# One flat list of single-engine steps in a new order, with every PSUM bank named by its step, for a windowed attention that feeds a gated two-layer MLP

## The chip, the cores and the metric

The kernel runs on one core of a Trainium2 chip. The metric is the device time of one execution in microseconds. Several runs are given by their median. A profile is one execution by itself; its span runs from its first to its last instruction.

## What is computed

Eight batches of eight heads, 576 positions and 64 columns a head. Each position attends to itself and the 63 before it. The result, 4608 tokens of 512 columns, goes through two matrices with a gated activation between them.

```python
scores = scale * np.matmul(q, k.transpose(0, 1, 3, 2))
mask = (rel >= 0) & (rel < 64)             # rel = query position - key position
attn = softmax(np.where(mask, scores, -1e9))
x = np.matmul(attn, v).transpose(0, 2, 1, 3).reshape(B * S, H * D)
h = x @ w_in                               # 512 -> 2048
g = h * (1.0 / (1.0 + np.exp(-1.702 * h)))
return (g @ w_out).astype(np.float32)      # 2048 -> 512
```

## The kernel before

**Units of work.** A block m (0 to 35) is 128 tokens, two groups of 64 queries. A chunk is four blocks. For a block: `scores` (L319) multiplies q and k of all heads into PSUM, `exp` (L333, L335) is ACT's, `mask` (L339) is DVE's, `pv` or `pv_two` (one block or two, L347) multiplies by v, `norm` (L363, L365) or `norm_two` (L391, L392) divides on DVE and writes `xs`. `xs` is then turned into `xT`: up to block 15 by TensorE (`x_mm`, `x_mm_two`) and a copy on ACT, from block 16 on by a DMA transpose on SP's queue (`x_dma`, L437).

**The MLP.** An up unit (`up_mm`, L453) takes w_in and `xT` and fills one PSUM bank: four groups of 128 features by 128 tokens up to chunk 2, two by 256 after. It is emptied by one gelu on ACT (`up_gelu`, L484) or by a tanh on ACT and a product on DVE (`up_th` L464, `up_g` L479). Chunk 0 goes down by plain products (`down`, L491). Every later half chunk q (2 to 17) goes down in seven products of a Winograd form of Strassen's scheme, each of eight matmuls (`product`, L568). Products 1, 6, 7 and 4 add up in one bank, the chain, which is copied out after 1, 6 and 7 (`keep_chain`, L113) before the next may write; products 2, 5 and 3 use a second bank, each followed by an add into the output tile (`add_out`, L593); `last_of_chain` copies the chain's end. Sums of gT and of w_out are made by DVE (`add_g` L544, `add_w` L528). Chunk 8 does its up part with the same scheme (`up_product` L668, `up_keep`, `up_add` L685, `up_last` L694, sums in `add_u` L635 and `add_x` L645).

**Transfers.** Batches 0, 1 and part of 2 come as fp32, are cast by POOL, DVE or ACT, and q and k are turned by TensorE or, in batch 2, by DMA. From (2, 3) on `load_bf16` (L228, L229) loads q, k and v with a cast from POOL's queue; `turn_dma` (L240) turns q and k into qt and kt on SP's queue; `shift_v` (L233, L235) makes a copy of v shifted by 64 rows on POOL, and waits for the v it copies. `store` (L584) writes an output tile, on SP's queue for the first twelve half chunks.

**Order.** The schedule is manual: each engine executes its instructions in the order in which the program makes them, and each step waits for its operands and buffers. Up to chunk 1 the order is Python calls written out; after that a text `plan` is read step by step, a letter and numbers each. Several letters stand for steps of several engines: `u32.g` is an up unit and its gelu, `l3.0` three loads, `y2.3` two transposes, `h2.3` two shifts, `t10` the transposes of a block pair with both copies. The queue of a store follows from the half chunk.

**Banks and buffers.** Eight PSUM banks: S (two), T (two), H (two, taken in turn) and O (two, taken in turn). In the plan up units use H, products O; `pv_two` takes one H bank for its eighth head; scores marked `.h` use both H banks. Output tiles come from one pool of five buffers in turn.

Of the kernel before, what the change touches and what calls it, by code (L numbers as in the profile page):

```python
# [29 lines left out]
def kernel(  # L30
# [20 lines left out]
    ob_pool = ctx.enter_context(tc.tile_pool(name="ob", bufs=5))  # L51
    psS = ctx.enter_context(tc.tile_pool(name="psS", bufs=1, space=bass.MemoryType.PSUM))
    psT = ctx.enter_context(tc.tile_pool(name="psT", bufs=1, space=bass.MemoryType.PSUM))
    psH = ctx.enter_context(tc.tile_pool(name="psH", bufs=2, space=bass.MemoryType.PSUM))
    psO = ctx.enter_context(tc.tile_pool(name="psO", bufs=2, space=bass.MemoryType.PSUM))
# [30 lines left out]
    def load_v(b, i, queue=None):  # L86
        (queue or nc.sync).dma_start(
            out=heads(stage_of_v(b, i)[0 : size(i), :]), in_=rows_of(v, b, i)
        )

    def cast_v(b, i, engine=None, parts=(0, 1, 2)):
        n, vn, vo = size(i), v_nat[b % 2], v_off[b % 2]
        src = heads(stage_of_v(b, i)[:])
        pieces = [
            (vo[64:128, i, :, 0:D], src[0:64]),
            (vn[0:n, i, :, 0:D], src[0:n]),
            (vo[0:64, i + 1, :, 0:D], src[64:128]) if i < 4 else None,
        ]
        for p in parts:
            if pieces[p]:  # L100
                (engine or nc.gpsimd).tensor_copy(out=pieces[p][0], in_=pieces[p][1])
# [4 lines left out]
    def load_qk(b, i):  # L106
        for w, src in enumerate((q, k)):
            nc.sync.dma_start(
                out=heads(stage_of_qk(b, i)[0 : size(i), w, 0:DM]), in_=rows_of(src, b, i)
            )  # L110
# [4 lines left out]
    def cast_qk(b, i):  # L115
        n = size(i)
        for w in range(2):
            nc.gpsimd.tensor_copy(
                out=rows[b % 2][w][0:n, i, :], in_=stage_of_qk(b, i)[0:n, w, 0:DM]
            )  # L120

    def load_quads(half):
        hs = slice(4 * half, 4 * half + 4)
        for w, src in enumerate((q, k)):
            nc.sync.dma_start(
                out=stage_qk[half][:, w, :].rearrange("p (h e) -> p h e", h=4),
                in_=src[0, hs, 0:512, :].rearrange("h (p r) d -> p h (r d)", r=4),
            )
# [37 lines left out]
    def load_pairs(b, i):  # L166
        n = pairs(i)
        for w, src in enumerate((q, k)):
            nc.sync.dma_start(
                out=stage_qk[(3 * b + i) % 2][0:n, w, :].rearrange("p (h e) -> p h e", h=H),  # L170
                in_=src[b, :, 256 * i : 256 * i + 2 * n, :].rearrange(
                    "h (p r) d -> p h (r d)", r=2
                ),
            )
# [17 lines left out]
    def turn_mm(b, i, w, tiles):  # L192
        n = pairs(i)
        for hp in range(4):
            for r in range(2):
                nc.tensor.transpose(  # L196
                    out=tiles[hp // 2][:, w, hp % 2, r, 0:n],
                    in_=pair_rows(b, i, w)[0:n, hp // 2, r, P * (hp % 2) : P * (hp % 2) + P],
                    identity=ident[0:n, 0:n],
                )  # L200

    def turn_out(b, i, w, tiles, half, engine):
# [6 lines left out]
            in_=tiles[half][:, w, :, :, 0:n].rearrange("p g r n -> p g n r"),  # L209
        )  # L210

    def turn_tiles():

        return [
            pool.tile([P, 2, 2, 2, P], bf16, name="turn", tag=tag)
            for pool, tag in ((psS, "S"), (psT, "T"))
        ]

# [7 lines left out]
    def load_bf16(b, i):  # L226
        for w, src in enumerate((q, k)):
            nc.gpsimd.dma_start(out=heads(row_block(b, i, w)), in_=rows_of(src, b, i))  # L228
        nc.gpsimd.dma_start(out=v_nat[b % 2][0 : size(i), i, :, 0:D], in_=rows_of(v, b, i))  # L229

    def shift_v(b, i):
        vn, vo = v_nat[b % 2], v_off[b % 2]
        nc.gpsimd.tensor_copy(out=vo[64:128, i, :, :], in_=vn[0:64, i, :, :])  # L233
        if i < 4:
            nc.gpsimd.tensor_copy(out=vo[0:64, i + 1, :, :], in_=vn[64:128, i, :, :])  # L235

    def turn_dma(b, i):
        n = size(i)
        for w in range(2):
            nc.sync.dma_start_transpose(  # L240
                out=qkt[b % 2][w][:, :, PAD + P * i : PAD + P * i + n],
                in_=row_block(b, i, w),
            )
# [15 lines left out]
    for half in range(2):  # L259
        load_quads(half)  # L260
    for i in (0, 2):
        load_v(0, i)
    ident = keep.tile([P, P], bf16, name="ident")
    nc.gpsimd.memset(ident[:], 0.0)
    nc.gpsimd.affine_select(
        out=ident[:], in_=ident[:], compare_op=ALU.not_equal, fill=1.0,
        base=0, pattern=[[-1, P]], channel_multiplier=1,
    )
    band = keep.tile([P, 64], bf16, name="band")
    nc.gpsimd.memset(band[:], 1.0)  # L270
    nc.gpsimd.affine_select(
        out=band[:], in_=band[:], compare_op=ALU.is_ge, fill=0.0,
        base=64, pattern=[[1, 64]], channel_multiplier=-1,
    )
    nc.gpsimd.affine_select(
        out=band[:], in_=band[:], compare_op=ALU.is_ge, fill=0.0,
        base=-1, pattern=[[-1, 64]], channel_multiplier=1,
    )
    for i in range(2):
        nc.vector.memset(qkt[i][1][:, :, 0:PAD], 0.0)  # L280
        nc.vector.memset(v_off[i][0:64, 0, :, :], 0.0)
        nc.vector.memset(v_nat[i][:, :, :, D : D + 2], 2.0)
        nc.vector.memset(v_off[i][:, 1:5, :, D : D + 2], 2.0)
        nc.vector.memset(v_off[i][64:128, 0, :, D : D + 2], 2.0)

    band_all = keep.tile([P, 1024], bf16, name="band_all")
    nc.vector.tensor_copy(
        out=band_all[:].rearrange("p (n c) -> p n c", c=64),
        in_=band[:].unsqueeze(1).to_broadcast([P, 16, 64]),
    )  # L290
    far = keep.tile([P, 512], bf16, name="far")
    nc.vector.tensor_scalar(
        out=far[:], in0=band_all[:, 0:512],
        scalar1=-1.0, scalar2=30000.0, op0=ALU.add, op1=ALU.mult,
    )
# [6 lines left out]
    def scores(m, masked=False, apart=False):  # L302

        if apart:
            st = [psH.tile([P, 512], fp32, name="S", tag="H")[:] for _ in range(2)]
# [67 lines left out]
    def pv_two(m):  # L373

        acc = psT.tile([P, 2, 512], fp32, name="Tacc", tag="T")
        rest = psH.tile([P, 2, 66], fp32, name="Tacc", tag="H")
# [27 lines left out]
    def x_dst(m):  # L404
        ch = m // 4
        if m % 4 == 0:
# [21 lines left out]
    def x_out_two(m):  # L428
        ps = X_of.pop(m)
        for i in range(2):  # L430
            nc.scalar.copy(out=x_dst(m + i), in_=ps[:, i])

    def x_out(m):
        nc.scalar.copy(out=x_dst(m), in_=X_of.pop(m)[:])
# [7 lines left out]
    turns = itertools.count()  # L442

    def up_mm(ch, f, nf, t0, nt, wide=False):

        pool, tag = (psO, "O") if wide and next(turns) % 2 else (psH, "H")
        ps = pool.tile([P, nf, nt], fp32, name="hps", tag=tag)

# [37 lines left out]
    def down(ch, tsub, j, pool=None, tag="O"):  # L486

        if j == 0:
            O_of[ch, tsub] = (pool or psO).tile([P, DM], fp32, name="ops", tag=tag)
# [9 lines left out]
    def down_out(ch, tsub, on_dve=False):  # L499
        o_sb = ob_pool.tile([P, DM], fp32, name="o_sb", tag="o_sb")  # L500
        ps = O_of.pop((ch, tsub))
        if on_dve:
            nc.vector.tensor_copy(out=o_sb[:], in_=ps[:])
        else:
            nc.scalar.copy(out=o_sb[:], in_=ps[:])
        eng = nc.sync if ch < 6 else nc.scalar
        eng.dma_start(out=out_tiled[:, ch * 4 + tsub, :], in_=o_sb[:])
# [40 lines left out]
    def bank(c, pr, at, name):  # L548
        pool, tag = (psO, "O") if (c, pr) != (NCH - 1, 1) else ((psS, "S"), (psT, "T"))[at]
        return pool.tile([P, 256], fp32, name=name, tag=tag)  # L550

    def product(c, pr, n):
# [8 lines left out]
        if n == 1:  # L561
            A_of[c, pr] = bank(c, pr, 0, "chain")
        if n == 2:
            C_of[c, pr] = bank(c, pr, 1, "part")
# [11 lines left out]
    def out_half(c, pr, t, n):  # L576
        if (c, pr, t) not in o_of:
            o_of[c, pr, t] = ob_pool.tile([P, DM], fp32, name="o_sb", tag="o_sb")
        return o_of[c, pr, t][:, 256 * n : 256 * n + 256]

    def store(c, pr, t, half=None):
        eng = nc.sync if c < 6 or half == 1 else nc.scalar
        cols = slice(0, DM) if half is None else slice(256 * half, 256 * half + 256)
        eng.dma_start(  # L584
# [6 lines left out]
    def add_out(c, pr, n):  # L591
        at, t, half = {2: (0, 0, 0), 5: (2, 1, 1), 3: (1, 0, 1)}[n]
        nc.vector.tensor_tensor(  # L593
            out=out_half(c, pr, t, half), in0=C_of[c, pr][:], in1=kept(c, pr, at), op=ALU.add
        )

    def last_of_chain(c, pr, engine):
        copy_on(engine, out=out_half(c, pr, 1, 0), in_=A_of.pop((c, pr))[:])
# [49 lines left out]
    rings = itertools.count()  # L648
    homes = {32: "ST", 33: "H", 34: "ST", 35: "H"}

    def up_bank(g, at):
        pool, tag = (psH, "H") if homes[g] == "H" else ((psS, "S"), (psT, "T"))[at]
        return pool.tile([P, 2, 256], fp32, name="up", tag=tag)[:]

    def up_product(g, n):
# [523 lines left out]
```

The softmax here doesn't subtract the row's maximum and nothing guards it: scores larger than these inputs give would overflow.

## Time and profile before

| what | value |
|---|---|
| runs | 295.73, 296.1 and 293.69 us, median 295.73 |
| the profiled execution | span 293.0 us; what lies around the span is not recorded |
| granted TensorE clock | 0.998 of full speed |
| first down product | 33.4 us |
| last matmul ends | 289.7 us |
| DMA packets | 149768, of which 135136 under 512 B; 42.79 MB |

Busy time is given by engine: PE is TensorE's matmuls, PEld its weight loads, DVE VectorE, ACT ScalarE, POOL GpSimd, SP SyncE, which here only issues transfers. A q behind a name means the sequencer of that engine. Groups are named by line, engine, operation and tiles; a wait is named by who waited and who ended it.

### The profile page before, as it was taken

What the parts mean: (1) busy time and instruction counts of PE and PEld (TensorE: products, weight loads), DVE (VectorE), ACT (ScalarE), POOL (GpSimd) and SP (SyncE); (2) the same over time, 40 slices, a digit from 0 to 9 for tenths busy, and PEclk for the clock granted to TensorE, in tenths of its full rate; (3) what the DMA queues carried; (4) which work ended last, traced back from release to release, by engine and by line L of the source; (5) the groups of instructions that cost most, each with busy time, mean ns of one, the idle gap of its engine ahead of it and who ended that gap; (6) DMA issues with size and microseconds to landing.
All of it is one profiled execution on the core that took longest, in us unless ns stands there. A gap on an engine that the chain in (4) does not pass through costs nothing.

```text
span 293.0 us, 8976 instructions
## 1 busy us (share of the span) xinstructions
PE 283.5 (97%) x3783; PEld 249.6 (85%) x3783; DVE 195.5 (67%) x377; ACT 181.1 (62%) x289; POOL 141.3 (48%) x191
## 2 busy tenths in 40 slices
PE   7899999999999999999999999999999999999995
PEld 6578555999898898889898999998899899989984
DVE  5667715898898685375636573756787864768771
ACT  3676534877775389776758746776657653556411
POOL 1570446744999999709569985078510000000000
PEclk9999999999999999999999999999999999999999
DMA  7999999996999999999999999999955171001233
GB/s 237 236 206 219 240 243 225 239 159 128 84 142 119 166 130 134 185 164 146 140 186 154 139 151 198 183 160 143 142 70 117 36 182 39 0 2 72 74 125 126
DMA packets 149768, 42.79 MB, mean 146 GB/s; under 512 B 135136, under 2 KB 144864, under 8 KB 149728
## 3 DMA queue, kind: packets, MB, share of 16 engines
q0 software_dynamic: 77712, 13.64, 70.7%
q1 hardware_dynamic: 68208, 25.18, 49.4%
q10 hardware_dynamic: 3808, 3.41, 3.7%
q8 instruction: 29, 0.48, 0.7%
q14 instruction: 11, 0.09, 0.1%
HBM read 36.70 MB, written 9.44 MB: 157 GB/s over the span
## 4 chain that ended last, share of the span: by engine, by line
PE 78%; DMA 10%; DVE 4%; ACT 2%; SPq 2%; issue 2%; POOL 1%; ACTq 0%; DVEq 0%; POOLq 0%
PE hps L453 32%; PE chain L568 17%; PE part L568 13%; PE ops L491 5%; PE up L668 4%; DMA out_dram<-o_sb 3%; PE Tacc L347 3%; PE S L319 3%; DMA kt<-rows_k 3%; DMA stage_v<-in_v_dram 2%; DMA stage_qk<-in_k_dram 2%; SPq L240 1%; DVE stage_qk L528 1%; ACT PT L335 1%; PE turn L196 1%
## 5 line engine op out<-in xcount | busy, mean ns | idle before, releaser
L453 PEld LDWEIGHTS <-w_in_sb 128*128 128x128 bf16 x1312 | 109.6, 113 | 4.9 <-issue 0.7
L484 ACT ACTIVATE gT<-hps 128x512 bf16<-128x512 f32 x82 | 48.6, 597 | 34.5 <-PE hps L453 34.2
L453 PE MATMUL hps<-xT_pe,w_in_sb 128*128 128x128 bf16 (+2 forms) x800 | 61.0, 234 | 0.1
L453 PE MATMUL hps<-xT_dma,w_in_sb 128*128 128x256 bf16 x512 | 60.6, 273 | 0.3 <-ACT gT L694 0.3
L568 PEld LDWEIGHTS <-gT 128*128 128x128 bf16 x512 | 49.0, 98 | 5.9
L479 DVE SCALAR_TENSOR_TENSOR gT<-th,hps 128x512 bf16<-128x512 bf16 x46 | 30.8, 684 | 11.2 <-ACT th L464 11.0
L233 POOL COPY v_off<-v_nat 64x528 bf16<-64x528 bf16 x27 | 20.2, 752 | 33.9 <-DMA v_nat<-in_v_dram 33.1
L464 ACT ACTIVATE th<-hps 128x512 bf16<-128x512 f32 x46 | 27.0, 600 | 13.0 <-PE hps L453 12.6
L593 DVE TENSOR_TENSOR o_sb<-part,stage_v 128x256 f32<-128x256 f32 x48 | 20.2, 421 | 21.9 <-PE part L568 13.3
L335 ACT ACTIVATE PT<-S 128x1024 bf16<-128x1024 f32 x28 | 28.5, 1017 | 8.0 <-PE S L319 7.6
L339 DVE TENSOR_TENSOR PT<-PT,band_all 128x1024 bf16<-128x1024 bf16 x32 | 23.6, 748 | 5.6 <-ACT PT L335 5.4
L229 POOL DMA_DIRECT2D v_nat<-in_v_dram x27 | 23.5, 871 | 0.8 <-DMA rows_q<-in_q_dram 0.5
L228 POOL DMA_DIRECT2D rows_k<-in_k_dram x27 | 23.3, 865 | 0.3 <-DMA v_nat<-in_v_dram 0.3
L228 POOL DMA_DIRECT2D rows_q<-in_q_dram x27 | 23.1, 856 | 0.0
L568 PEld LDWEIGHTS <-sums 128*128 128x128 bf16 x192 | 18.6, 98 | 3.2 <-issue 1.1
L568 PEld LDWEIGHTS <-stage_v 128*128 128x128 bf16 x192 | 18.5, 98 | 2.2
L113 ACT COPY stage_v<-chain 128x256 f32<-128x256 f32 x22 | 8.2, 372 | 18.3 <-PE chain L568 18.3
L392 DVE TENSOR_TENSOR xs<-Tacc,rc 128x128 bf16<-128x128 f32 (+1 forms) x26 | 18.0, 692 | 0.9
L113 DVE COPY stage_v<-chain 128x256 f32<-128x256 f32 x26 | 10.9, 420 | 11.1 <-PE chain L568 10.9
L235 POOL COPY v_off<-v_nat 64x528 bf16<-64x528 bf16 x21 | 17.2, 820 | 1.2
L568 PE MATMUL chain<-stage_qk,sums 128*128 128x256 bf16 x128 | 16.6, 273 | 0.3 <-DVE stage_v L113 0.3
L568 PE MATMUL chain<-stage_qk,gT 128*128 128x256 bf16 x128 | 16.6, 273 | 0.0
(127 smaller groups left out, 450.6 us busy)
## 6 DMA issues: line engine op xcount, KB each, us to landing
out_dram<-o_sb SPq DMA_DIRECT2D x24, 256.0 KB, 4.7
rows_q<-in_q_dram POOLq DMA_DIRECT2D x21, 128.0 KB, 6.3
rows_k<-in_k_dram POOLq DMA_DIRECT2D x21, 128.0 KB, 6.7
v_nat<-in_v_dram POOLq DMA_DIRECT2D x21, 128.0 KB, 7.4
out_dram<-o_sb ACTq DMA_DIRECT2D x10, 256.0 KB, 2.1
stage_v<-in_v_dram SPq DMA_DIRECT2D x9, 256.0 KB, 6.7
stage_qk<-in_q_dram SPq DMA_DIRECT2D x4, 512.0 KB, 6.9
stage_qk<-in_k_dram SPq DMA_DIRECT2D x4, 512.0 KB, 8.0
```

The source lines that it names most:

```text
L113: (nc.scalar.copy if engine is nc.scalar else engine.tensor_copy)(**kw)
L228: nc.gpsimd.dma_start(out=heads(row_block(b, i, w)), in_=rows_of(src, b, i))
L229: nc.gpsimd.dma_start(out=v_nat[b % 2][0 : size(i), i, :, 0:D], in_=rows_of(v, b, i))
L233: nc.gpsimd.tensor_copy(out=vo[64:128, i, :, :], in_=vn[0:64, i, :, :])
L335: nc.scalar.activation(out=e[:], in_=st[:], func=AF.Exp, scale=scale)
L339: nc.vector.tensor_tensor(out=pt, in0=pt, in1=band_all[:], op=ALU.mult)
L453: nc.tensor.matmul(ps[:, g, :], lhsT=w_in[:, c, (f + g) % 4 : 512 : 4], rhs=xT[ch][:, m0 : m0 + nt // P, c, :], start=(c == 0), stop=(c == 3),
L464: nc.scalar.activation(out=th[:], in_=ps[:], func=AF.Tanh, scale=1.702)
L479: nc.vector.scalar_tensor_tensor(out=g_of(*unit), in0=th[:], scalar=1.0, in1=ps[:], op0=ALU.add, op1=ALU.mult,)
L484: nc.scalar.activation(out=g_of(*unit), in_=ps[:], func=AF.Gelu_apprx_sigmoid, scale=2.0)
L568: nc.tensor.matmul(out[:, :], lhsT=left[:, j], rhs=right[:, j], start=new and j == 0, stop=j == 7, skip_group_check=True,)
L593: nc.vector.tensor_tensor(out=out_half(c, pr, t, half), in0=C_of[c, pr][:], in1=kept(c, pr, at), op=ALU.add)
```

## The change

The whole order, start included, becomes one text of 1291 steps, each of one engine (a transposing step, a load of q alone, one half of a shift, one copy). The order up to the first down product is that of before; from there on it is new. The H and O pools become four pools of one bank each, a to d, and each step that starts a bank says which. The five output buffers become five pools e to i, named by the step that first writes a tile. Queues of stores and engines of copies are named too. Each step does the arithmetic that it did before; where a gelu and where a tanh with a product empties an up unit is chosen anew.

```diff
-    ob_pool = ctx.enter_context(tc.tile_pool(name="ob", bufs=5))
+    ob0 = ctx.enter_context(tc.tile_pool(name="ob0", bufs=1))
...
+    obs = {"e": ob0, "f": ob1, "g": ob2, "h": ob3, "i": ob4}
-    psH = ctx.enter_context(tc.tile_pool(name="psH", bufs=2, space=bass.MemoryType.PSUM))
-    psO = ctx.enter_context(tc.tile_pool(name="psO", bufs=2, space=bass.MemoryType.PSUM))
+    psA = ctx.enter_context(tc.tile_pool(name="psA", bufs=1, space=bass.MemoryType.PSUM))
...
+    pools = {"S": psS, "T": psT, "a": psA, "b": psB, "c": psC, "d": psD}
-    def up_mm(ch, f, nf, t0, nt, wide=False):
-        pool, tag = (psO, "O") if wide and next(turns) % 2 else (psH, "H")
-        ps = pool.tile([P, nf, nt], fp32, name="hps", tag=tag)
+    def up_mm(ch, f, nf, t0, nt, tag):
+        ps = pools[tag].tile([P, nf, nt], fp32, name="hps", tag=tag)
-    def shift_v(b, i):
+    def shift_v(b, i, part):
-    def turn_dma(b, i):
+    def turn_dma(b, i, w):
-    def load_bf16(b, i):
+    def load_bf16(b, i, which):
-    def store(c, pr, t, half=None):
-        eng = nc.sync if c < 6 or half == 1 else nc.scalar
+    def store(c, pr, t, half, queue):
-        "t": turn,
-        "c": lambda m, *apart: scores(m, apart=bool(apart)),
+        "X": lambda m, tag: x_mm(m, pools[tag], tag),
+        "XX": lambda m, tag: x_mm_two(m, pools[tag], tag),
+        "Y": lambda m, e: x_out(m, engines[e]),
+        "YY": lambda m, i, e: x_out_two(m, i, engines[e]),
+        "xd": x_dma,
```

In the new text `u.6.12.2.256.256.d` is an up unit (chunk, feature group, groups, first token, tokens, bank), `e` its gelu, `t` and `g` its tanh and product; `p.11.1.a` a product; `k`, `o`, `z` its copies and add; `v.26.2.a` the attention product of two blocks; `n` the norm; `c` scores (two letters: banks apart), `x` exp, `m` mask; `XX` transposes on TensorE, `YY` their copies, `xd` a DMA transpose of xs; `lb` a load, `y` a DMA transpose of q (0) or k (1), `h` half a shift, `s` a store, `a` a sum of gT. Three places of before and after: block pair 12 up to its transposes, block pairs 14 and 16, and from block pair 26 to the first up unit that uses it.

```diff
-        a3.2 a3.4 c12 x12 p2.4 o2.5 p2.3 z2.V p3.1 o2.3 h3.3 k3.1.V m12 p3.2 o3.2 h3.4 c13 x13 p3.6
-        k3.6.A p3.5 p3.7 m13 y3.4 k3.7.V o3.5 v12 c14 p3.4 z3.A x14 n12 p3.3 t12 p4.1 c15 x15 y4.0
+        m.13 v.12.2.a z.2.A.g n.12.2 p.3.4 p.2.5 XX.12.T y.3.4.1 y.3.4.0 o.3.5.h y.3.3.1 z.3.V
+        lb.4.0.q YY.12.0.V o.2.5 YY.12.1.A y.3.3.0 c.14 c.15.ac x.15 y.4.0.1 x.14 p.3.3 a.5.3 p.2.3
...
-        m15 s2.0 s3.0 m14 c16 x16 v14 n14 m16 c17.h x17 l4.2 p4.5 p4.6 k4.6.V t14 m17 u54.g p4.7 v16
-        n16 c18 l4.3 t16 h4.0 l4.4 u55.g u56.g u57.g u58.g k4.7.V o4.5 u59.t g59 u60.g p4.3 o4.3
+        h.3.1.1 e.3.10.0 h.3.3.0 e.3.4.0 e.3.8.0 k.4.1.A c.17.ca c.16 x.17 s.2.0.N.S v.14.2.d n.14.2
+        h.3.4.0 y.4.0.0 p.4.6 u.3.12.2.0.256.d lb.4.3.k k.4.6.V y.4.1.1 XX.14.T YY.14.0.V p.4.2.c
...
+        u.3.0.2.256.256.b m.17 o.4.2.e u.3.12.2.256.256.a x.16 m.16 y.4.4.0 h.3.3.1 v.16.2.d
+        lb.4.2.q e.3.12.0 a.6.3 a.6.1 y.4.3.1 c.18 z.4.A.i a.6.2 a.5.2 y.4.2.0 e.3.6.256 lb.4.3.v
+        e.3.2.256 s.3.0.N.S e.3.0.256 h.4.4.0 e.3.12.256 c.19.ba x.19 lb.5.2.k n.16.2 p.4.5 xd.16
+        xd.17 o.4.5 lb.4.1.v s.4.1.N.S p.5.1.d k.5.1.A y.4.3.0 m.19 u.3.14.2.256.256.b t.3.14.256
+        g.3.14.256 p.5.6 k.5.6.V u.3.8.2.256.256.a t.3.8.256 g.3.8.256 p.4.3 o.4.3 p.5.7 k.5.7.V
...
-        y7.1 y7.0 k9.6.V u97.g u98.g m28 l7.2 p9.7 k9.7.A u99.g o9.2 v26 l7.3 s5.1 a10.1 n26 y6.3
-        c29 a10.2 x29 u100.g u101.g p9.4 z9.V p9.5 p10.1 o9.5 t26 p9.3 u102.g k10.1.V p10.6 k10.6.A
+        k.10.7.A p.9.3 y.6.2.0 v.26.2.a c.29 x.29 c.31.bd x.31 s.6.0.N.S o.9.3 n.26.2
+        u.6.8.2.0.256.a p.10.4 p.10.2.b m.29 h.6.3.0 u.6.0.2.0.256.d o.10.2.e p.10.5 z.10.V.f
+        e.6.8.0 lb.6.4.v o.10.5 y.7.1.0 e.6.0.0 h.6.1.1 s.8.0.N.S h.6.0.1 v.28.2.a h.7.0.0 y.6.3.0
+        c.30 y.7.1.1 c.32.cd x.32 x.30 p.10.3 lb.7.3.v n.28.2 o.10.3 m.32 xd.27 p.11.1.a aw.1.0
+        lb.7.4.q u.6.14.2.0.256.c k.11.1.A aw.1.1 xd.26 m.30 e.6.14.0 a.12.3 u.6.12.2.256.256.d
```

## The prediction

> **What bounds the kernel now.** I read the page first, then the busy time by stage, then the waits of TensorE, then the chain of waits at single places, and last the rows by shape for the prices.
>
> ```profile
> span 293.0 us, 8976 instructions
> ...
> PE 283.5 (97%) x3783; PEld 249.6 (85%) x3783; DVE 195.5 (67%) x377; ACT 181.1 (62%) x289; POOL 141.3 (48%) x191
> ...
> PE   7899999999999999999999999999999999999995
> ...
> PEclk9999999999999999999999999999999999999999
> DMA  7999999996999999999999999999955171001233
> ```
>
> TensorE (PE) is busy in every slice, at full clock. The DMA engines are as full until slice 30 (220 us). By stage, the columns being length, then PE, PEld, DVE, ACT, POOL:
>
> ```profile
> 33.40:65.00 31.60, 31.60 (x470) 22.63 (x469) 20.15 (x38) 18.89 (x34) 18.71 (x28) 1.00 1.07 224
> 65.00:120.00 55.00, 54.48 (x919) 49.58 (x917) 43.66 (x78) 38.93 (x60) 49.73 (x63) 1.00 1.84 128
> 120.00:200.00 80.00, 79.39 (x991) 72.89 (x989) 46.19 (x91) 56.95 (x86) 51.34 (x65) 1.00 1.88 164
> 200.00:245.00 45.00, 44.51 (x587) 41.14 (x585) 33.08 (x64) 27.88 (x45) 8.92 (x12) 1.00 0.77 106
> 245.00:289.70 44.70, 44.33 (x405) 40.64 (x403) 30.77 (x65) 18.47 (x38) 0.00 (x0) 1.00 0.17 63
> ```
>
> From the first down product (33.4 us) to the last matmul (289.7) there are 256.3 us, of which PE is drawn busy 254.3. A busy PE hides part of each stall: matmuls of 256 columns follow each other every 109 ns (the chain of waits gives 0.87 us for eight), but each is drawn 273 ns long, so a stall is drawn 0.164 us too short. I went through the PE timeline by the distance between starts. Eight stalls exceed 0.15 us: at 77.6 (0.27 us, ended by DVE's mask), 81.7 (0.23, DVE's tanh product), 91.0 (0.46, DVE's kept chain), 112.1 (0.25, DVE's norm), 123.4 (0.65, DVE's output add), 144.3 (0.29, ACT's exp), 204.4 (0.66, a DMA into kt) and 256.8 (0.49, ACT's gelu): 3.30 us. That agrees with 2.0 drawn idle plus 8 x 0.164. TensorE's own waits show the longest four after the start:
>
> ```profile
> PE S L319 <- DMA kt<-rows_k: 0.5, 1, 0.5
> PE part L568 <- DVE o_sb L593: 0.5, 1, 0.5
> PE hps L453 <- ACT gT L694: 0.3, 1, 0.3
> PE chain L568 <- DVE stage_v L113: 0.3, 1, 0.3
> ```
>
> One of them, in the chain of waits, is a store that landed late, held a buffer, and so an add and a PSUM bank:
>
> ```profile
> 114.31 8.47 DMA out_dram<-o_sb
> 122.78 0.03 issue
> 122.81 0.02 DVEq L593
> 122.83 0.04 issue
> 122.88 0.44 DVE o_sb L593
> 123.31 0.04 issue
> 123.35 1.03 PE part L568 x8
> ```
>
> So an order can win 3.3 us at most: 33.4 us of start, 253.0 of flow and 3.3 of tail (289.7 to 293.0) make 289.7 us.
>
> [...]
>
> **The change part by part.**
> *Work.* Counting both lists step by step: 112 products, 128 up units, 28 Winograd up products, 16 down steps, 36 scores, 36 exps, 81 POOL loads, 60 + 20 DMA transposes, 34 + 4 stores in both. PE's flow stays 253.0 us. Four gelus replace tanh and product pairs: ACT 0, DVE -4 x 0.684 = -2.7 us. Scores in two banks are four more: ACT +4 x (2 x 0.587 - 1.017) = +0.6. Turns between gelu and exp tables go from 29 to 31: ACT +2 x 1.283 = +2.6. Seven casts and copies go between POOL, ACT and DVE, 0.6 each. ACT and DVE have 11 to 34 us idle in each stage after 65 us, so I take 0 for all; without that cover each queued step would delay PE by its 0.6 to 1.3 us. Before the first down product the order is unchanged and only bank names differ: 0, with +-0.3 as its ends.
> *Stalls removed.* I looked at each of the eight in the new list. 77.6: score 10 comes 2.9 us of PE work before its product instead of score 11's 2.0, for an exp and mask of 1.2 + 0.75 plus waits: gone. 81.7: the unit is now gelu alone: gone. 91.0: the kept copy is on ACT and the next product 13 us of PE work later: gone. 112.1: scores 17 take banks c and a, not the bank of the norm: gone. 123.4: the buffers of that stretch are named and their stores lie 10 us of PE work or more ahead of reuse: gone. 144.3: bank d was read long before: gone. 256.8: the next unit takes bank a, two steps after an add: gone. 204.4 is a transfer and stays open. Gain: 3.30 - 0.66 = 2.64 us.
> *Stalls added, certain ones.* The transposes XX.12 and XX.14 follow their attention products v.12 and v.14 after two steps of eight 256-column matmuls (2 x 0.87 = 1.74 us of cover); before it was these and one score (2.16). They wait for the whole norm: its four parts take 0.169 + 0.291 + 0.237 + 1.092 = 1.79 us by the rows of L391 and L392, plus 0.16 that a matmul outlasts its flow and some 0.1 of semaphores, 2.05 us. Each falls short by 0.3: +0.6 us. Queued behind on PE is all else.
> *Transfers.* From 16 on, a block goes v, norm, two SP transposes (L437), first up unit. PE's cover from v to that unit was 14.4 to 20.5 us for chunks 4 to 7; now it is 10.5, 13.0, 11.7, 11.3, 13.5, 9.6, 14.4, 15.3. The 9.6, for blocks 26 and 27, is four scores (4 x 0.42), eight steps of 0.87 and one pair of attention products (0.9). The tile view prices the transposes:
>
> ```profile
> L437 SPq DMA_TRANSPOSE xT_dma<-xs x20: 1190/1248/2342, 118.7 to 236.9; - x20
> ...
> DMA to landing us min/median/max: 2.4/5.9/8.8
> ```
>
> Needed are 2.05 + 1.25 + landing: 9.2 us at the median, 12.1 at the worst, if SP is free. SP has other work: y transposes stand ahead (1.2 us each, and each waits for its own load), and one lies between the pair 20 and 21. At the median all eight hold. With the latencies of before at those moments (about 8.0 at 119 us, 7.1 to 7.7 at 199, 3.5 to 4.3 at 205) blocks 16 lack 11.3 - 10.5 = 0.8, and blocks 26 lack 0 to 1.2, 0.6 in the middle. I take +1.4, with 0 and +6.6 (worst landing on four of them: 1.6 + 1.7 + 0.8 + 2.5) as ends. The 0.66 of the open stall I put inside this: score 30 comes 3 us of PE work later, but its q transpose stands behind two stores and another transpose on SP. POOL's loads are split and shuffled with the shifts; a shift that waits for its v holds every load behind it. The last loads of batch 7 wait behind the shift of 7.3, whose v waits for product 26 (about 200 us); counted at 3.5 us a load, as at 210 us in before, the last k and q are turned near 219 us for scores due at 225: 6 us of cover, so 0.
> *Tail.* Before it ends in a copy (0.37) and an ACT store; after in an add (0.42) and an SP store: +0.05, taken as 0.
> *Sum.* -2.64 + 0.6 + 1.4 - 0.6 (of the 1.4, the part that stood already at 204.4) = -1.24, about -1.2. From the span of 293.0: 291.8. The page does not show what lies around the span; the median of the runs is 2.73 us above it, and I move the difference there: 295.73 - 1.2 = 294.5 us.
>
> **The rivals.** *No stall is left.* For it: each of the eight has its cause removed, and the busiest helper is 67% busy. Against: the 0.6 counted. Time: 295.73 - 3.3 = 292.4. *The stalls move.* DMA is full until 220 us in any order and PE waits for it elsewhere: what is won is lost again, 295.7, with 295 to 298 as its width. For it: loads of 8 to 13 us at 165 to 180; against: only one of eight stalls is a load. *The shorter cover before the up units ends on late transposes* (slower). Four edges at the worst landing cost 6.6 us: -2.64 + 0.6 + 6.6 + 0.66 = +5.2, 300.9 us. It decides against the change from a sum of 2.0 us of lateness on. For it: 9.6 to 11.7 us of cover against 12.1 needed; against: the median landing. *The change does nothing* is excluded as a case of its own: PE's order differs right from the first down product.
>
> **How the numbers follow.** Small gain (293 to 295): 0.40. No stall left (291 to 293): 0.27. Stalls move (295 to 298): 0.17. Late transposes (298 to 302): 0.16. The likeliest gives 294.5. Its own range is 293 to 296; the one for all is 291.2 to 299.5. A difference over 1% (about what a measurement can tell) means below 292.8 or above 298.7. Faster takes the second case and the edge of the first: 0.30. Slower takes most of the last: 0.17. Within: 0.53.
>
> **What would show it.** PE busy near 253 us of flow as before, stalls at XX.12 and XX.14 of 0.3 us, ended by DVE's xs; none at an output add near 123 us; waits of an up unit for xT near 125 and 210 us under 1.5 us. The SP list's xT wait and the POOL shifts' wait for v_nat tell whether transfers are later. I am wrong if PE waits over 3 us in sum for xT, kt or qt, or if the sum of PE's stalls is below 1 us.

## The result and the profile after

The changed kernel takes 291.2 us (median of four runs, 290.84 to 291.8) where the kernel before takes 294.9 beside it (293.69 to 296.1): a ratio of 0.987, with a 95% interval of 0.982 to 0.991. That is 3.7 us less, where 1.2 were forecast. In some executions here, three of the traces among them, TensorE's clock averages 0.83 of full speed from 10 to 20 us and everything after starts 1 to 1.8 us later; ratios leave out runs more than 1.5% above the fastest of their kernel. Traces are compared below by the stretch from the first down product to the end of the last matmul, which leaves a late start out: 256.25 us before, 252.84 after.

The head of the page of the changed kernel (its own time is 291.29 us, 1.7 more than its span):

```profile
span 289.6 us, 8951 instructions
...
PE 280.6 (97%) x3776; PEld 250.2 (86%) x3783; DVE 196.6 (68%) x379; ACT 187.3 (65%) x302; POOL 132.9 (46%) x185
```

Seven of the 3783 matmuls have no record in this trace; they leave gaps of 0.2 to 0.3 us beside 512-column matmuls before 54 us, which are no waits. ACT is 6.2 us busier and DVE 1.1, and neither matters. By stage, with the columns of the prediction:

```profile
33.20:65.00 31.80, 31.03 (x462) 22.30 (x466) 22.53 (x43) 22.08 (x36) 17.93 (x28) 1.00 1.22 218
65.00:120.00 55.00, 53.96 (x890) 50.37 (x887) 43.21 (x77) 39.87 (x65) 43.98 (x58) 1.00 2.26 156
120.00:200.00 80.00, 80.00 (x1056) 74.20 (x1056) 46.99 (x93) 56.56 (x87) 46.31 (x60) 1.00 1.60 147
200.00:245.00 45.00, 45.00 (x582) 42.12 (x580) 33.53 (x65) 32.37 (x53) 11.58 (x16) 1.00 0.78 106
245.00:286.10 41.10, 41.05 (x377) 37.77 (x374) 28.22 (x62) 16.88 (x34) 0.00 (x0) 1.00 0.19 71
```

From 120 to 245 us TensorE doesn't stand still at all: 80.00 of 80 and 45.00 of 45, where the kernel before had 79.39 and 44.51. What waits are left lie before 84 us. Of TensorE's own waits, two are of this stretch:

```profile
PE S L318 <- DMA kt<-rows_k: 1.0, 1, 1.0
...
PE Tacc L346 <- DVE PT L338: 0.3, 1, 0.3
```

The first is score 12, and the chain of waits (start, length, what) shows its k leaving SP at 74.53 and landing 8.45 us later:

```profile
74.53 8.45 DMA kt<-rows_k
82.98 0.05 issue
83.02 0.41 PE S L318 x16
```

By the distance between starts, waits over 0.11 us are 3.44 us before (nine) and 1.78 after (0.45 at 56.2, 0.13 at 58.5, 1.20 at 83.0). So waits explain 1.66 of the 3.41 us. The larger surprise is the flow of the matmuls itself. The groups by shape show that attention runs the array in other tile shapes (rows*columns of the array that a matmul uses) than all else:

```profile
L559 PE MATMUL chain<-stage_qk,gT 128*128 128x256 bf16 x128 | 16.6, 273 | 0.0
...
L346 PE MATMUL Tacc<-v_off,PT 128*64 128x65 bf16 x320 | 13.7, 196 | 0.1
L318 PE MATMUL S<-qt,kt 64*128 64x64 bf16 x576 | 12.7, 191 | 1.2 <-DMA kt<-rows_k 1.0
```

Products use 128*128, scores 64*128, attention products 128*64. Each change from one shape to another costs about 0.1 us in which nothing waits for anything. By the distance between starts it is the same in the traces of both kernels: 0.205 us from a matmul of 256 columns to the first of a score and 0.202 to 0.203 to that of an attention product, where 0.109 leads to the next of its own kind; and 0.120 to 0.127 from a score or an attention product to another shape, where 0.05 at most leads to the next of its own kind (waits aside). TensorE's timeline of the changed kernel shows two scores side by side:

```profile
100.45 0.61 PE L423 MATMUL pxt<-ident,xs 128*128 128x128 bf16 x8
101.00 0.64 PE L318 MATMUL S<-qt,kt 64*128 64x64 bf16 x32
101.57 1.05 PE L559 MATMUL part<-w_out_sb,stage_v 128*128 128x256 bf16 x8
```

Eight transposes at 56 ns end at 100.90, and the next full matmul starts at 101.57: 0.67 us for two scores. A score by itself takes 0.436 in the same way, so a pair saves 0.20. Counted over the stretch (four changes to and from the 32*128 of a turn, the same in both, left out), the shape changes 80 times in the kernel before and 66 times after (scores stand in pairs eleven times where they did five times, and 14 runs of small matmuls join scores with an attention product where 11 did); without their waits these runs of small matmuls take 24.06 us before and 22.66 after. That is 1.40 us, 0.10 for each of 14 changes. 1.66 + 1.40 = 3.06; the other 0.35 of the 3.41 are waits under 0.11 us.

### The profile page after: what moved, and what is told of

It is laid out like the page before. It is cut to its first block, busy times and chain, and to the rows that moved or that the text cites. A ratio compares the mean times of both kernels' runs of the same rounds, so it can differ in the third digit from the quotient of the medians.

```text
span 289.6 us, 8951 instructions
## 1 busy us (share of the span) xinstructions
PE 280.6 (97%) x3776; PEld 250.2 (86%) x3783; DVE 196.6 (68%) x379; ACT 187.3 (65%) x302; POOL 132.9 (46%) x185
## 3 DMA queue, kind: packets, MB, share of 16 engines
q10 hardware_dynamic: 3808, 3.41, 3.8%
## 4 chain that ended last, share of the span: by engine, by line
PE 87%; DMA 7%; ACT 1%; POOL 1%; DVE 1%; issue 0%; SPq 0%; POOLq 0%
PE hps L447 37%; PE chain L559 19%; PE part L559 14%; PE up L658 4%; PE ops L485 4%; PE Tacc L346 4%; PE S L318 3%; DMA kt<-rows_k 3%; DMA stage_v<-in_v_dram 2%; DMA stage_qk<-in_k_dram 2%; PE turn L197 1%; PE pxt L414 1%; POOL v_off L117 1%; DVE PT L338 1%; POOL v_nat L117 0%; ACT L718 0%
## 5 line engine op out<-in xcount | busy, mean ns | idle before, releaser
L478 ACT ACTIVATE gT<-hps 128x512 bf16<-128x512 f32 x86 | 49.7, 597 | 30.8 <-PE hps L447 30.5
L447 PE MATMUL hps<-xT_dma,w_in_sb 128*128 128x256 bf16 x512 | 62.0, 273 | 0.0
L473 DVE SCALAR_TENSOR_TENSOR gT<-th,hps 128x512 bf16<-128x512 bf16 x42 | 28.4, 685 | 7.5 <-ACT th L458 7.4
L458 ACT ACTIVATE th<-hps 128x512 bf16<-128x512 f32 x42 | 24.7, 597 | 10.9 <-PE hps L447 10.7
L229 POOL DMA_DIRECT2D v_nat<-in_v_dram x27 | 22.8, 848 | 17.4 <-issue 17.1
L237 POOL COPY v_off<-v_nat 64x528 bf16<-64x528 bf16 x27 | 18.6, 697 | 24.7 <-DMA v_nat<-in_v_dram 24.2
L334 ACT ACTIVATE PT<-S 128x1024 bf16<-128x1024 f32 x24 | 24.4, 1016 | 4.3 <-PE S L318 4.1
L239 POOL COPY v_off<-v_nat 64x528 bf16<-64x528 bf16 x21 | 16.3, 791 | 10.0 <-DMA v_nat<-in_v_dram 9.6
L478 ACT ACT_TABLE_LOAD x14 | 18.0, 1283 | 0.2
L718 ACT ACT_TABLE_LOAD x13 | 16.7, 1283 | 0.2
```

What stands on the lines that cost most here:

```text
L334: nc.scalar.activation(out=e[:], in_=st[:], func=AF.Exp, scale=scale)
L447: nc.tensor.matmul(ps[:, g, :], lhsT=w_in[:, c, (f + g) % 4 : 512 : 4], rhs=xT[ch][:, m0 : m0 + nt // P, c, :], start=(c == 0), stop=(c == 3),
L458: nc.scalar.activation(out=th[:], in_=ps[:], func=AF.Tanh, scale=1.702)
L473: nc.vector.scalar_tensor_tensor(out=g_of(*unit), in0=th[:], scalar=1.0, in1=ps[:], op0=ALU.add, op1=ALU.mult,)
L478: nc.scalar.activation(out=g_of(*unit), in_=ps[:], func=AF.Gelu_apprx_sigmoid, scale=2.0)
```

## The experiments

Theory T: of the 3.4 us won, about 2 are waits that went and 1.4 are shape changes saved. R1: only waits count, the flow is the same in any order. R2: a mended wait comes back elsewhere, as one for a transfer. R3: the transfers are the bound where the new order left less cover. The table leaves out four runs that tell little, which are told below; ratios are to the kernel before on the same chip.

| kernel | median us | ratio, 95% interval | stretch in its trace |
|---|---|---|---|
| before, on six chips | 294.8 to 295.8 | 1 | 256.25, 257.29 |
| changed, again | 290.9 | 0.987, 0.983 to 0.992 | 252.55 |
| scores parted, 8 places | 292.7 | 0.992, 0.990 to 0.995 | 255.15 |
| scores parted from attention products, 13 | 296.4 | 1.006, 1.003 to 1.008 | 258.72 |
| score 12 late | 291.7 | 0.990, 0.986 to 0.994 | 253.37 |
| score 12 beside 13 | 292.0 | 0.990, 0.986 to 0.994 | 252.44 |
| changed, spare transposes | 300.6 | 1.017, 1.013 to 1.021 | 259.59 |
| before, spare transposes | 305.9 | 1.037, 1.032 to 1.042 | 267.65 |
| before, stores early | 295.0 | 1.001, 0.998 to 1.003 | 256.81 |
| before, four waits mended | 298.9 | 1.014, 1.010 to 1.018 | 257.77 |
| the same, k of score 30 early | 295.6 | 1.001, 0.998 to 1.004 | 256.67 |
| the same, k of score 15 early too | 296.2 | 1.003, 0.999 to 1.007 | 257.73 |
| before, those loads alone | 295.0 | 0.998, 0.995 to 1.000 | 256.53 |

**The changed kernel again.**

> The changed kernel once more, so that the kernels beside it have it on their own chip. Both theories: 290.8 to 291.8 us, 1.2 to 1.5% below the kernel before (294.9).

290.9 us. Its waits lie elsewhere than in the first trace: 0.56 us at score 10 and 0.18 at score 12, both for late transposes, and 0.63 at 89.5 us for nothing that the profile shows. Gaps without a releaser stand in three more traces of this kernel's family: 1.05 and 0.87 us (scores parted), 1.39 and 0.52 (score 12 late), 1.32 (scores parted from attention products), all before 86 us. TensorE's timeline, for the gap at 89.5:

```profile
89.49 0.80 PE L447 MATMUL hps<-xT_pe,w_in_sb 128*128 128x128 bf16 x11 [0.47 <-issue]
```

What TensorE waits for in these six gaps is not shown; no edit tests it.

**Shape changes: scores parted.** Eight times, in this manner:

```diff
-c.14 c.15.ac x.15 y.4.0.1 x.14 p.3.3 a.5.3
+c.15.ac x.15 y.4.0.1 p.3.3 c.14 x.14 a.5.3
```

> Eight places where two scores stand side by side on TensorE are parted by one product step or up unit that stood beside them; nothing else moves but what hangs on the later score. Theory T (of the 3.4 us won about 1.4 us come from fewer changes between the small matmuls of attention and the full ones, at about 0.20 us for each run that disappears): eight runs more, 26 to 34, so +1.6 us over the changed kernel, 292.8 us, with TensorE idle no longer than before. Rival R1 (all of the gain is waits that went; the flow of the matmuls is the same in any order): 0, 291.2 us, unless a score that comes 0.9 us later adds a wait, which the distances between starts would show.

292.7, so +1.8 us over the changed kernel; T said +1.6, R1 nothing. The trace has 82 shape changes, 16 more, and the runs of small matmuls take 24.30 us without their waits, 1.64 more than 22.66. The stretch is 2.60 longer than in the trace above: this execution, the slowest of nine, also holds two of the gaps without a releaser, 1.92 us where that one had 1.37 of waits. One of the places in TensorE's timeline:

```profile
101.72 0.41 PE L318 MATMUL S<-qt,kt 64*128 64x64 bf16 x16
102.06 1.05 PE L559 MATMUL part<-w_out_sb,stage_v 128*128 128x256 bf16 x8
103.04 0.41 PE L318 MATMUL S<-qt,kt 64*128 64x64 bf16 x16
103.38 1.05 PE L559 MATMUL part<-w_out_sb,sums 128*128 128x256 bf16 x8
```

Eight matmuls at 109 ns from 102.06 end at 102.93; the score starts 0.11 later, and nothing is named as its releaser. R1 has fallen.

**Scores parted from attention products.** Thirteen places, such as

```diff
-v.26.2.a c.29 x.29 c.31.bd x.31 s.6.0.N.S o.9.3 n.26.2 u.6.8.2.0.256.a
+v.26.2.a s.6.0.N.S o.9.3 n.26.2 u.6.8.2.0.256.a c.29 x.29 c.31.bd x.31
```

> The changed kernel with thirteen places, at which a score stands right beside an attention product on TensorE, parted by one product step or up unit from beside them; scores that stand beside scores stay so. Theory T: the trace of the changed kernel gives 1.07 us for one score and two attention blocks together and 0.44 + 0.73 = 1.16 apart, so about 0.10 us a place, 13 x 0.10 = +1.25 us, against 0.20 for a parting of two scores. R1 (flow is the same in any order): 0.

The flow is as expected: 79 changes, 13 more, and 23.92 us, 1.26 more. The time is not: +5.5 us. The rest are fifteen waits of 0.15 to 0.56 us, 4.6 in sum, and one gap without a releaser (1.32). Most of the waits are for DVE or ACT, whose work now comes some 0.9 us later for a product that needs it at once, as in TensorE's waits:

```profile
PE hps L447 <- DVE xs L391: 0.7, 3, 0.3
```

A parted score also stops covering the norm: the unit that takes the bank of v.14 waits 0.25 us, and XX.14 0.41. So standing together pays twice in this order, by the flow and by these waits.

**Score 12.** Its exp stood behind score 13 already.

```diff
-y.2.3.1 c.12 h.3.0.0
...
+u.2.4.4.384.128.b c.12 p.2.6
```

> Score 12 alone is moved some 8 us later on TensorE, behind up unit 4 of chunk 2, last quarter, and five steps ahead of score 13, whose PSUM bank it shares; its exp stood behind score 13's place anyway. Theory T (a wait for a late k is all that is lost there): in executions in which score 12 waited (1.20 us in one, 0.18 in the next) the wait is gone, so -0.2 to -1.2 us against the changed kernel (290.9), and no other wait over 0.3 us takes its place. Rival R3 (the transfers are the bound there): score 13 or a later score waits instead, 0.

The wait for k is gone and no other score waits, but the one trace has two of the gaps without a releaser (1.39 us at 76.7 and 0.52 at 85.0). The runs fall into three at 290.3 to 290.6 and three, at a mean clock of 0.992 or 0.993 and in the trace with the late start told of above, at 292.8 to 293.8: 0.3 to 0.6 us better at most, which these runs don't resolve. Directly ahead of score 13 it was worse placed:

> Score 12 is moved from the place where it waited 1.2 us for its k (83.0 us) to right ahead of score 13; its exp already stood behind score 13. Theory T: the wait goes (-1.2) and two runs of small matmuls become one (-0.2): -1.4 us against the changed kernel, 289.8 us. R1: -1.2, 290.0. Rival R3 (the transfers are the bound in this stretch and TensorE waits for the next one instead): 0 to -0.3.

The k is in time, but both scores use PSUM bank S, so the second waits 1.28 us for the exp of the first. I had overlooked the bank; the run says nothing on R3.

**Two gelus by tanh again** (`e.1.4.0` and `e.1.0.0` become `t` and `g`).

> Two of the gelus of chunk 1 (first quarters of units 4 and 0) are made by tanh and a DVE product again, as before the change: two changes of ACT's table less, two DVE products of about 0.68 us more. If the wait of 0.45 us of attention product 6 at 56.2 us hangs on ACT's table loads ahead of exp 6: -0.4 us, 290.8. If it hangs on DVE's queue: 0 to +0.5.

292.1 us, ratio 0.991 (0.988 to 0.994), runs from 290.4 to 294.6. The wait aimed at was in the first trace of the changed kernel only, not in the second, so this run tells nothing.

**Is the shorter cover a weakness?** First each xT transpose was made twice into the same tile:

```diff
-        nc.sync.dma_start_transpose(out=x_dst(m), in_=xs_of.pop(m))
+        xs = xs_of.pop(m)
+        for _ in range(2):
+            nc.sync.dma_start_transpose(out=x_dst(m), in_=xs)
```

> The changed kernel with each DMA transpose of xT made twice (the second writes the same data over the first), so that SP has 20 more transposes of about 1.2 us and each pair of blocks has its xT some 2.5 us later; the result is the same. Tests the shorter cover that the prediction feared (10.5, 13.0, 11.7, 11.3, 13.5, 9.6, 14.4 and 15.3 us from the attention product to the first up unit). From the changed kernel's landings (6.3, 5.3, 4.9, 6.6, 3.6, 4.3 us): blocks 16 need 1.5 + 5.0 + 6.3 = 12.8 us, 20 need 11.4, 22 need 13.1, 26 need 10.8. If the prediction's account of cover is right and only the landing was over-priced: TensorE waits at blocks 16, 22 and 26, in sum +3 to +6 us. If up units are covered by something else: under +1.

> The same doubling in the kernel before, whose cover is 14.4 to 20.5 us: 0 to +1 us over the kernel before, by the account of cover. If SP's time or the load on the DMA engines by itself is what costs: the same loss as in the changed kernel.

339.8 and 339.2 us: four transposes hold SP for 15.19 us (121.16 to 136.4), where each is 1.20 us of issue at the median and takes 2.4 to 7.5 us to land, and what SP issues behind them is late (in the old order TensorE waits 8.0 us for an output add and up to 4.9 for a k). That the second write waits on SP for the first to land is my reading of it. Far from a delay of 2.5 us, so nothing is told apart. With a buffer of its own for the spare one:

```diff
+        spare = spare_pool.tile([P, 3, P], bf16, name="spare", tag="spare")
+        nc.sync.dma_start_transpose(out=spare[:], in_=xs[:, 0:384])
+        nc.sync.dma_start_transpose(out=x_dst(m), in_=xs)
```

> The changed kernel with a spare DMA transpose ahead of each transpose of xT: three quarters of the same block into a buffer of its own that nobody reads, so no transpose waits for another's landing and the output is unchanged. Each pair of blocks gets its xT about 1.9 to 2.5 us later. In two executions of the changed kernel xT landed ahead of its first up unit by 0.4 and 0.6 us (blocks 16), 1.1 and 0.8 (18), 2.4 and 1.2 (20), 1.9 and 3.4 (22), 2.7 and 2.4 (26), 1.4 and 2.1 (28), 5 or more (24, 30). If the cover is what the trace says: waits of 1.4 to 2.0 us at blocks 16, 0.8 to 1.7 at 18, 0 to 1 at 20 and 28, in sum +2.2 to +5 us. If xT is not on the path: under +0.5.

> The same spare transposes in the kernel before, where xT landed ahead of its first up unit by 4.1 us (blocks 16), 0.7 (18), 3.8 (20), 4.5 (22), 3.8 (24), 4.4 (26), 10 or more (28, 30). By the trace: a wait of 1.2 to 1.8 us at blocks 18 alone, so +1.2 to +2. If the load on SP and the DMA engines by itself is what costs: as much as in the changed kernel.

The changed kernel loses 9.7 us, the kernel before 11.1; by the stretches of the traces, about 7 and 11.4. TensorE's longest wait, of the changed kernel and then of the one before:

```profile
PE hps L451 <- DMA xT_dma<-xs: 6.1, 5, 2.2
```

```profile
PE hps L457 <- DMA xT_dma<-xs: 5.5, 3, 2.3
PE S L320 <- DMA kt<-rows_k: 2.3, 1, 2.3
```

In the changed kernel blocks 16 lost 2.4 us, 18 1.1, 20 0.3 and 22 0.8, and blocks 26, for which I expected nothing, 2.4. For the kernel before I expected 1.2 to 2 and was far off: with the spare transposes on SP TensorE also waits 2.3 us for a k and 1.4 for an output add. The waits for xT are about as long in both, 6.1 and 5.5 us, and the whole loss is not greater in the new order. So the shorter cover before the up units is no weakness that shows here, and R3 falls for xT; it says nothing on k and q.

**Do mended waits come off the end?** First the store at 123 us, by putting four stores ahead on SP:

```diff
-m15 s2.0 s3.0 m14
...
+o2.3 s2.1 s2.0 h3.3
```

> The kernel before with four stores (two of group 2, two of group 3) moved up on SP to right behind the step that fills their buffer, so that the output add at 123 us finds its buffer free. Nothing else moves. Theory T (a wait that goes in the middle comes off the end): the wait of 0.65 us is gone and the time is 0.65 us shorter than before. Rival R2 (waits move on, since transfers are full there): the wait is gone, a later one takes its place, 0.

The wait is gone, and the time is the same. In the trace 0.45 us come back 4 us later, at 127.6, where a product waits for a copy that stands behind sums on DVE: a wait for an engine, not for a transfer. Also, score 15 waits 1.11 us for its k at 105.1, whose transpose took 8.62 us from issue to landing; it was issued at 96.5, before the moved stores (102.0), so the edit did not delay its issue. Whether the stores slowed its last 3 us is not shown. A second trace of the untouched kernel shows what varies anyhow:

> The kernel before once more, for a second trace of it: its waits for engines (0.46 us at 91.0, 0.23 at 81.7, 0.25 at 112.1, 0.65 at 123.4, 0.29 at 144.3, 0.49 at 256.8) should return in size, since they follow from the order; its waits for transfers (score 15 with 1.4 us to spare, score 30 with none and a wait of 0.66) may vary by a microsecond. From the first down product to the end of the last matmul 256.3 us by theory T, within 0.7.

Its waits for engines return, but for the one at 123.4 (behind a store) and with 0.35 for 0.46 at the kept chain; block 18 waits 1.43 us for xT at 148.4. Then four waits were mended one by one:

```diff
-k2.6.V
+k2.6.A
-u37.t g37
+u37.g
-s2.0 s3.0
+s2.0 y4.1
-c17.h x17 l4.2 p4.5
+l4.2 p4.5 c17.h x17
```

> The kernel before with four of its waits mended one by one and its order otherwise kept: a kept chain on ACT (wait of 0.46 us at 91.0), one up unit by gelu alone (0.23 at 81.7), one store ahead of one y transpose on SP (0.65 at 123.4), score 17 one product later (0.25 at 112.1, less about 0.1 for a run of small matmuls that is parted). Theory T (waits are one part of the gain and come off the end one for one): 0.46 + 0.23 + 0.65 + 0.15 = 1.5 us shorter than before, 293.5. Rival (a wait that goes comes back later as another): 0.

All four are gone from the trace, but score 15 waits 1.0 us and score 30 2.4 for their k. The time can't be used: the mean clock of all six runs is 0.987 to 0.994, and the trace has the late start. Next, the load and turn of score 30 were put ahead of those of batch 7. A first form also moved score 15 two units later:

> The four waits mended as in the kernel before it, and the two scores whose k came late there helped: score 15 two units later on TensorE, the load and the transposes for score 30 ahead of those of batch 7 on POOL and SP. From the first down product to the end of the last matmul: the kernel before has 256.25 us. Theory T (waits are 2 of the 3.4 us and come off the end once no late k takes them up): 256.25 - 1.6 - 0.66 = 254.0 us, 1.2 above the changed kernel, which is what its flow saves. Rival (the transfers set the end in that order, whatever score waits): 256 or more, with waits of 1 us or more for kt elsewhere. Median time if the start is as before: 292.6 by T, 295 by the rival.

298.4 us: exp 15 then stood between two gelus, with two more table loads (1.28 us each), and a unit waited 3.14 us for its bank. After that idle time the granted clock itself is lower (by stage: length, busy times, clock, DMA share, GB/s):

```profile
110.00:115.00 5.00, 2.02 (x14) 1.53 (x13) 1.29 (x2) 4.18 (x7) 5.00 (x7) 0.89 2.11 142
115.00:120.00 5.00, 5.00 (x91) 3.90 (x90) 2.66 (x6) 3.87 (x6) 4.84 (x8) 0.76 2.15 136
```

TensorE is drawn idle for 2.98 us, until 113.18; the clock is 0.89 in the stage that holds this, 0.76 in the next and 1.00 from 120 us on. In the second trace of the untouched kernel it is 1.00 in all three, and in the kernel below, which has no such wait, 1.00 from 65 to 120 us. Whether the idle time itself is the cause is not shown. Without that move:

> As the last one, but score 15 stays where it was: moved between two units it put its exp between two gelus, cost two changes of ACT's table (1.28 us each) and so a new wait of 3.1 us. From the first down product to the end of the last matmul: theory T 256.25 - 1.6 (four waits for engines) - 0.66 (k of score 30) = 254.0 us, and up to 1.0 us more where score 15 waits for its k, as it did in two of five traces of this order: 254 to 255. Rival (a wait that goes in this order comes back at the transfers): 256 or more.

Here five waits of the kernel before, 0.46 + 0.23 + 0.25 + 0.65 + 0.66 = 2.25 us, are gone from the trace, and over 20 runs the time is that of the kernel before: a ratio of 1.001, with an interval that leaves room for 0.7 us of gain and not for 2.25. In the trace score 15 waits 1.72 us for k and block 18 0.66 for xT instead. The chain of waits, followed back from score 15:

```profile
84.90 1.10 POOL v_off L233
...
87.09 2.00 POOL v_off L233 x2
...
90.13 0.81 POOL rows_q L228
90.94 6.42 DMA rows_k<-in_k_dram
...
97.41 7.58 DMA kt<-rows_k
...
105.04 0.29 PE S L319 x8
```

Shift copies hold POOL from 84.9 to 90.1, the load behind them takes 6.42 us, the transpose behind that 7.58. Score 15 had 1.4 us to spare in both traces of the untouched kernel, and the landing varies by more than that: from the start of its load to the landing of k it took 11.94 us in the first of these traces (90.92 to 102.86) and 14.05 here (90.94 to 104.99). The mended waits ahead of it, 0.23 and 0.46 us, take up more of what it had to spare. So that load was put ahead of the shifts, with the mended waits and without:

```diff
-h2.3 h2.4 y3.0 h3.0 y2.4 l3.2
...
+l3.2 h2.3 h2.4 y3.0 h3.0 y2.4
```

> The last kernel (four waits for engines mended in the old order, k of score 30 early), and one load more moved: that of rows 2 of batch 3, on which score 15 waited 1.7 us in the last trace, stands ahead of three pairs of shift copies on POOL that held it from 84.9 to 90.1 us, and so comes some 4 us earlier. From the first down product to the end of the last matmul: theory T2 (waits for engines come off the end, but only where k comes early enough behind them) 256.7 - 1.7 = 255.0 us at most and 254.0 at best, median time 293.3 to 294.0. Rival (a transfer sets the end in this order in any case): 256 or more, 295.5.

> The three moves of loads and transposes alone (rows 2 of batch 3, rows 3 of batch 6 and their turn), without the four mended waits. T2: only the wait of 0.66 us of score 30 was one for k, so -0.7 us, 294.9; together with the one before, neither half alone gives what both give. If the loads are the whole matter: as good as both together, -1.6 to -2.3 us.

Neither gains what it should. In the first, score 15 is in time, but the shift that now comes later holds attention product 10 (1.68 us at 79.0), and scores 13 and 31 wait for k (0.61 and 1.30); in the second, score 31 waits 1.10 and an output add 0.70. In both, loads moved ahead by hand came with others that were late. In the old order R2 holds as far as it was tried: the time stays, whichever waits are mended, and what comes back is mostly a wait for a transfer. A form in which they come off by local edits was not found.

The new order spaces the transfers anew. From each trace, the time from the landing of the last k or q that a score needs to the score: score 15 had 1.4 us before, 4.9 and 4.2 in the two traces after; score 30 had none, now 9.3; only scores 10 and 12 have under 0.1 us in one trace or both, and there the waits are. That this spacing is what lets mended waits come off is the reading that fits all runs; no single edit shows it by itself.

## Why the prediction was wrong, step by step

The forecast of no measurable change was wrong: 1.2 us were expected and 3.7 came. Of the miss of 3.3 us in the time itself, 0.8 is that the median of the kernel before was 295.73 in three runs and is 294.9 in four; the rest is in the sum. (The prediction put 2.73 us between span and time; in every run that gives both it is 1.7.)

*Work: "PE's flow stays 253.0 us".* This is the step that failed. The products, units and scores on TensorE were counted rightly, but their neighbours weren't looked at, so the flow was held fixed without a reason, and with it the bound of 3.3 us on what an order can win. The flow shrank by 1.40 us, 14 shape changes at 0.10, and the two partings confirm the price (1.64 us for 16, 1.26 for 13). What the array does in this time the traces don't show. The shapes were in the rows by shape of the kernel before:

```profile
L319 PE MATMUL S<-qt,kt 64*128 64x64 bf16 x576 | 14.0, 191 | 0.6 <-DMA kt<-rows_k 0.5
```

On ACT the count was off: 29 and 31 turns between tables were counted, the traces have 22 table loads before and 28 after, of 1283 ns each. It made no difference: ACT's and DVE's extra work cost nothing, as the step said.

*Stalls removed, -2.64.* All seven went, and the eighth (204.4) too. They are gone from both traces of the new order; other waits, 1.78 and 1.37 us in sum, stand elsewhere. That a wait that goes comes off the end was assumed, though, and in the old order it doesn't: four of the seven and the eighth, mended, gave 0.

*Stalls added, +0.6.* Nothing came. The price took the norm as starting when the attention product ends; its first parts run while the second block is still multiplied, as DVE's timeline shows (that product's matmuls run to 98.70):

```profile
98.36 0.17 DVE L390 RECIPROCAL rc<-Tacc 128x2 f32<-128x2 f32 x1 [1.16 <-PE Tacc L346]
...
99.11 1.09 DVE L391 TENSOR_TENSOR xs<-Tacc,rc 128x896 bf16<-128x896 f32 x1
```

(The 0.1 for semaphores was an estimate; the chain at 122.78 us has 0.10 from a store's landing to the add behind it.) So some 1.5 us of cover are needed and not 2.05; XX.12 starts at 100.45, 0.25 after the norm's end. With 1.74 of cover that is close, as the wait at XX.14 in the second parting shows.

*Transfers, +1.4.* The up units waited 0. The landings were taken from the kernel before at the same moments, and they are shorter in the new order: 6.2 us for 8.0 at blocks 16, 3.4 to 4.3 for 7.1 to 7.7 at blocks 26. xT came 0.35 us ahead of its unit at blocks 16 and 2.7 ahead at 26, where shortfalls of 0.8 and 0.6 were priced; over all DMA transposes of xT:

```profile
DMA to landing us min/median/max: 2.5/3.9/7.1
```

Instead a score came late for its k (1.20 us), at a place that the prediction did not look at because it lies before block 16. Size nearly right, place wrong: that the size fits is luck. (The loads issued from 165 to 180 us, which the prediction puts at 8 to 13 us, took 9.1 to 12.9 from issue to landing; transfers from SP took 7.1 to 9.1 there.)

*Start and tail, 0.* Right: 33.2 us for 33.4, and 3.5 for 3.3. *The last loads, 0.* Right: scores 33 to 35 had 1.4 us or more.

*The sum.* -1.40 (not seen), -1.66 (net of all waits over 0.11 us; predicted -1.24) and -0.35 of shorter waits make -3.41. That the term of the waits came near is luck too: the +0.6 did not come, the eighth stall went, and the late transfer stood elsewhere. *The rivals.* "No stall is left" came nearest with 292.4, but for a reason that isn't so: 1.4 to 1.8 us of waits are left, and the flow gave the difference. "The stalls move" is what happens to edits of the old order. "Late transposes" is excluded by the traces of the changed kernel, in which no up unit waits for xT.

## What to carry to other kernels

Count the changes of the matmul's tile shape in an order as well as its matmuls, at 0.10 us each here: where small-tile work is woven into full-tile work, put it side by side as far as banks and operands allow. In the old order 2.25 us of mended waits left the time as it was, with 1.4 us to spare at a transfer behind some of them; so list for each consumer how long ahead of it its operand landed, and look for the smallest of these before pricing a gain. In the new order moves of 0.9 us at thirteen places brought fifteen waits, 4.6 us in sum. Count gaps without a releaser, 0.5 to 1.4 us each in four traces here, apart from waits.

## What had not been expected of the hardware

A change of tile shape between 128*128, 64*128 and 128*64 costs 0.10 us each way, with no wait named in the trace. In a trace with 3.0 us of idle time in mid kernel (until 113.18) the clock was 0.76 from 115 to 120 us. Four DMA transposes, every second of which writes over the target of the one ahead of it, held SP's queue for 15.19 us, where each is 1.20 us of issue. Six gaps of 0.5 to 1.4 us on TensorE, all before 90 us, have no releaser in the trace.
